# Two attention layers on one core: another order of the running maxima in plain steps, and two loads moved by a step

## The chip, the core and the metric

The kernel runs on one core of a Trainium2 chip. The metric is the device time of one execution, in microseconds (us); a run here means the median over several executions. A core has five engines with queues of their own, which work side by side and wait for one another through semaphores: PE (matmuls; its weight loads are shown as PEld), DVE (reductions and elementwise work), ACT (activation functions), POOL (elementwise work) and SP, which here issues nearly all of the DMAs. [...]

## The reference

Two attention layers, each over 2048 positions with 576 features, 32 heads of 18. Layer A looks at 8 positions behind each query, every second one; layer B is full attention. The outputs stand side by side.

```python
def _A_ref(x, wqkv, wo):
    B, S, D = x.shape
    H = 32; Dh = D // H
    W, dil = 8, 2
    qkv = (lambda x, *d: x.transpose(*d))((x @ wqkv).reshape(B, S, 3, H, Dh), 2, 0, 3, 1, 4)
    q, k, v = qkv[0], qkv[1], qkv[2]
    scale = Dh ** -0.5
...
    idx = pos[:, None] - off[None, :]
...
    logits = jnp.einsum("bhsd,bhswd->bhsw", q, kg) * scale
    logits = jnp.where(mask[None, None, :, :], logits, -1e9)
    attn = _softmax(logits, axis=-1)
    o = jnp.einsum("bhsw,bhswd->bhsd", attn, vg)
    return (lambda x, *d: x.transpose(*d))(o, 0, 2, 1, 3).reshape(B, S, D) @ wo

def _B_ref(x, wqkv, wo):
...
    scores = jnp.einsum("bhqd,bhkd->bhqk", q, k) * scale
    p = _softmax(scores, axis=-1)
    o = jnp.einsum("bhqk,bhkd->bhqd", p, v)
    return (lambda x, *d: x.transpose(*d))(o, 0, 2, 1, 3).reshape(B, S, D) @ wo
...
return jnp.concatenate([a, b], axis=-1)
```

## The kernel before

The first 420 us compute the projections (q, k, v of both layers) and the first 516 of 2048 maximum matmuls. After that the program is a loop of 512 steps, written out by hand. The 32 heads of layer B are taken in 8 groups g of four heads; a group has 4 blocks of 512 queries; a block has 16 steps, one for each 128 keys. Block n = 4 g + b begins at step 16 n. The work of a step:

- **Four scores** (`score`, line 305): for head h of the group a matmul of 56 rows, 128 keys against 512 queries. Head h uses the rows 64 r to 64 r + 55 of the array with r = h mod 2, so that two scores run side by side on the two row groups. Each score writes one of four PSUM banks ("scores"); ACT takes the exponential out of it into a tile `e` (line 309).
- **The weighing** (`weigh`, line 772) of the step before: four matmuls of the values with `e`, in two passes each, which use all rows and sum into the bank `po`. After 16 steps the sums leave through `finish`.
- **Maxima for later blocks.** The softmax needs the largest score of each query before its exponentials, so the same scores are computed ahead of time the other way round (queries on the partitions) and reduced by DVE. A *whole* maximum (`whole`, letters A for row group 0 and B for row group 1) is a matmul of 512 columns (line 175) into one of three PSUM banks ("else") and a reduction by DVE (lines 191 and 193). A *half* maximum (`part` through `first_part`, letters D and E) is done in a pair: D writes 256 columns of row group 0 into a bank, E writes 256 columns of row group 1 into the other half of the same bank, and one reduction (line 205) reads both. E's matmul stands behind a no-operation on PE (line 201) that waits until D's matmul is through.

What a step does in which order is a string: digits are scores, letters the maxima. Where nothing else is due, the step is *plain* and the string is `PLAIN` (line 50). Where local results are multiplied with their output weights (`sums_of_a`, lines 1104 on), there are four whole maxima and another order. PE works its queue in this order; the weighing follows the eight matmuls of the string.

When the last of a block's 64 maximum matmuls has been reduced (at step s), the maxima go on by an agenda of due steps: `least` (DVE, line 214) at s, `turn` (a transpose on DVE, line 222) at s + 1, `halve` (a split in two parts on POOL, line 112) at s + 2, `order` (line 232: two DMAs to DRAM, `dm<-mt`) two steps after that, and `place` (line 238: two DMAs back into the rows of the queries, `qs<-dm`) three steps later, in the last group one step later. The first score of the block needs them. By the order of the agenda, what was planned at the start stands before what is added on the way.

All these DMAs go through SP's queue, which issues them in the order of the program: an issue that waits for its semaphores holds up all behind it.

Layer A runs on POOL, DVE and ACT beside all this, in 8 portions j of 256 positions (`local`). A portion's results are written to DRAM by `put`, read again in halves n by `get` (lines 990 and 992: six DMAs, `at<-dao` and `ahl<-dao`, into tiles that exist once) and multiplied by `sums_of_a` in two later steps from the list `TURNS`. The step of `get` is the later of the step in which the tiles' last use before comes (or the results are in DRAM), `at`, and nine steps before the first use, `one - 9`.

Of the kernel before, what the change touches and what calls it, by code (L numbers as in the profile page):

```python
# [22 lines left out]
NG = H // 4  # L23
# [23 lines left out]

MORE = (439, 441, 451, 467, 475, 477, 484, 486)

PLAIN = "D1A30E2B"  # L50

GAP = 55

# [10 lines left out]
def rows(t, *dims):  # L64

    return bass.AP(tensor=t.tensor, offset=t.offset, ap=[list(d) for d in dims])
# [3 lines left out]
def two_attentions(ctx: ExitStack, tc, xa, wa, woa, xb, wb, wob, out):  # L70
# [19 lines left out]
    def bank(kind=None):  # L90
        r = rings[kind or ring]
        r.append(r.pop(0))
        return p_bank.tile([128, 512], F32, name=f"bank{r[-1]}")
# [17 lines left out]
    def split_on(engine, hi, lo, raw):  # L111
        engine.tensor_copy(hi, raw)  # L112
        engine.tensor_sub(lo, raw, hi)
# [5 lines left out]
    def later(n, f):  # L119
        agenda[step + n].append(f)  # L120
# [37 lines left out]
    def behind_of(later, *before):  # L158

        for b in before:  # L160
            tc.add_manual_dep(later.ins, b.ins.name,
                              mybir.DependencyInfo(mybir.DependencyClass.Sync, mybir.DependencyReason.DATA),
                              reason="in order")

    def block(g, b):

        qs, ks = sets[g % 3]
        mx = maxes.tile([128, 2, 2, 4, 6], F32, name="mx", bufs=3)
        left = 2 * 8 * 6
        rest = [[(k, t, p) for k in range(NB) for t in range(4) for p in range(2)] for _ in range(2)]  # L170

        def take(ps, r, k, t, p, at, n):

            rows_ = slice(64 * r, 64 * r + 54)
            return nc.tensor.matmul(ps, qs[rows_, b, p, 128 * t : 128 * t + 128],  # L175
                                    ks[rows_, p, 512 * k + at : 512 * k + at + n], start=True, stop=True)

        def made(n):
            nonlocal left
            left -= n  # L180
            if left == 0:
                later(int(projecting), least)

        def whole(r):
            k, t, p = rest[r].pop(0)
            ps = bank()
            take(ps, r, k, t, p, 0, 512)

            def reduce():
                if k < 2:  # L190
                    nc.vector.tensor_reduce(mx[:, r, p, t, k : k + 1], ps, axis=AX.X, op=ALU.max)  # L191
                else:
                    nc.vector.tensor_reduce(mx[:, r, p, t, 2 * k - 2 : 2 * k], ps.rearrange("q (h n) -> q h n", h=2),  # L193
                                            axis=AX.X, op=ALU.max)
                made(1 + (k > 1))

            return reduce

        def part(i, k, t, p, r, ps, before=None):
            if before:  # L200
                behind_of(nc.tensor.nop(nofuse=True), before)
            ins = take(ps[:, 256 * r : 256 * r + 256], r, k, t, p, 256 * i, 256)

            def reduce():
                nc.vector.tensor_reduce(mx[:, :, p, t, 2 * k - 2 + i], ps.rearrange("q (h n) -> q h n", h=2),  # L205
                                        axis=AX.X, op=ALU.max)
                made(2)

            return ins, reduce

        def least():
            m = least_rooms[n_least[0] % 2]
            n_least[0] += 1
            nc.vector.tensor_reduce(m[:, :16], mx.rearrange("q r p t k -> q (r p t) k"), axis=AX.X, op=ALU.max,
                                    negate=True)
            later(1, lambda: turn(m))

        def turn(m):

            parts = maxes.tile([128, 2, 32], F32R, name="mt", bufs=2)  # L220
            raw = parts[:, 1].bitcast(F32)
            nc.vector.transpose(raw, m)  # L222
            later(1, lambda: halve(parts, raw))

        def halve(parts, raw):
            split_on(nc.gpsimd, parts[:, 0], parts[:, 1], raw)
            later(2, lambda: order(parts))

        def order(parts):

            for k in range(2):
                load(rows(dm[g, b, k, 0, 0], (32, 4), (128, 32), (1, 32)), parts[:, k].bitcast(F32))
            later(1 if g == NG - 1 else 3, place)

        def place():
            placed.add((g, b))
            for k in range(2):
                load(qs.bitcast(F32)[54 + k : 128 : 64, b].rearrange("r p n -> r (p n)"),
                     dm[g, b, k, :16].rearrange("(r i) n -> r (i n)", r=2))

        return rest, whole, part
# [169 lines left out]
    with (tc.tile_pool(name="x", bufs=1, side="right") as xp,  # L411
# [103 lines left out]
        if True:  # L515
# [34 lines left out]
            for c in range(5):  # L550
                one, other = (load, nc.scalar.dma_start) if c % 2 == 0 else (nc.scalar.dma_start, load)
# [159 lines left out]
            for k in range(2, 14):  # L711
                n = 46 if k == 2 else 36 + 4 * k
# [7 lines left out]
            def leave_a(c, b, n, ps):  # L720
                o = xp.tile([128, 512], F32, name="ohi", bufs=4)
                nc.scalar.activation(o[:n], ps, AF.Copy)  # L722
                load(da[128 * c : 128 * c + n, HALO + 512 * b : HALO + 512 * b + 512], o[:n])


            order = [t for i in (0, 8) for j in range(4) for t in (i + j, i + j + 4)]
# [18 lines left out]
            order = [(c, b) for b0 in range(0, NB, 2) for c in range(2) for b in (b0, b0 + 1)]  # L745
            order += [(c, b) for c in range(2, 14) for b in range(NB)]
            for c, b in order:
                n = min(128, 3 * D - 128 * c)
                work_list.append(((b % 2, ws[c][0], xas[b][0], slice(0, n), every),
                                  lambda ps, n=n: ps[:n], lambda ps, c=c, b=b, n=n: leave_a(c, b, n, ps)))  # L750
# [135 lines left out]
    def local(j):  # L886
# [92 lines left out]
        def put(i):  # L979
            load(rows(dao[j, i, 0, 0], (DH * SUB, 128), (1, DH * SUB)),  # L980
                 ap(st["parts"][i].bitcast(F32), (1, DH * SUB)))

        def get(n):
            st["x"] = []
            st["n"] = n
            last = work.tile([128, 128], F32R, name="ahl", bufs=1)
            for i in range(2):
                t = work.tile([128, 4, 128], F32R, name=f"at{i}", bufs=1)
                for s in range(2):
                    load(t.bitcast(F32)[:, :, SUB * s : SUB * s + SUB],  # L990
                         dao[j, i, 2 * n + s, :512].rearrange("(c p) n -> p c n", p=128))
                load(last.bitcast(F32)[64 * i : 64 * i + 64].rearrange("p (s n) -> p s n", s=2),
                     rows(dao[j, i, 2 * n, 512], (SUB, 64), (D * SUB, 2), (1, SUB)))
                st["x"].append([t[:, c] for c in range(4)])
            st["x"].append(last)

        def finished(h):
            inside.append(lambda: sums_of_a(h))
# [18 lines left out]
        pieces = [(LOWER, lower), (SHARE, share), (UP, upper), (REST, rest), (PUT0, lambda: put(0)), (PUT1, lambda: put(1))]  # L1017
# [12 lines left out]
        start = A_FROM + GAP * j  # L1030
        for n in range(2):
            free, begin = turns[-1] if turns else 0, start + PUT1 + 5
            at = max(free, begin)
            one = next(t for t in TURNS if t >= at + 7)
            two = next(t for t in TURNS if t > one + 1)
            turns.extend((one, two))
            pieces.append((max(at, one - 9) - start, lambda n=n: get(n)))
            for h, t in enumerate((one, two)):
                pieces.append((t - 1 - start, lambda h=h: finished(h)))
                producing.add(t)  # L1040
            pieces.append((two + 5 - start, lambda n=n: load(out[p0 + 128 * n : p0 + 128 * n + 128, :D], ys["a", j, n])))
# [142 lines left out]
    for j in range(NJ):  # L1184
        plan(A_FROM + GAP * j, local(j))
# [40 lines left out]
    while step < ALL:  # L1226
        n, kt = divmod(step, NT)
        g, b = divmod(n, NB)
        many = min(4 if behind() > 0 else 3, total - int(sum(given)))
        if not inside and many in (1, 3):  # L1230
            order = PLAIN if many > 1 else PLAIN.replace("A", "").replace("B", "")
        else:
            places = positions(many)
            order = "".join("%d%s" % (h, "BA"[h % 2] if h in places else "") for h in range(4))
            if inside:
                at = order.index("3" if 3 in places else "2") if step % NT != AT or AT == 0 else FIRST
                order = order[:at] + "+" + order[at:]
# [56 lines left out]
```

## Time and profile before

| what | value |
|---|---|
| median of three runs | 1611.54 us (1610.16 to 1611.78) |
| the profiled execution, its own time | 1610.11 us |
| its span, first to last instruction | 1608.3 us |
| busy share of PE, DVE, ACT, POOL | 99%, 86%, 75%, 60% |
| granted TensorE clock | 0.999 |

The profile comes from one execution. A row of a timeline has the start and the length in us, the engine, the line of the kernel, the operation, the tiles (out<-in), the shapes and how many were merged; in brackets the idle time before it and what ended that. A row of a group has busy time, mean duration and idle time before. Busy times of PE rest on modelled ends of matmuls.

### The profile page before, as it was taken

The page shows a single profiled execution, that of the slowest core. Times are in us where ns is not written, and L with a number is a line of the kernel's source. Part 1 is how long each engine was busy: PE and PEld are TensorE (multiplying, and loading weights), DVE is VectorE, ACT ScalarE, POOL GpSimd, SP SyncE. Part 2 cuts the span into 40 slices and gives each one's busy share as a digit, 9 for nine tenths or more (in the row PEclk, how much of TensorE's full clock was granted, in tenths as well). Part 3 has the DMA queues.
Part 4 walks back from the last instruction along what each step waited for, and adds up shares of the span by engine and source line. Part 5 has one row for each costly group of instructions (what it writes and reads, how often), then busy time and mean ns, then how long its engine had stood idle before and what let it go on. Part 6 is the DMA issues. An engine that isn't in the chain of part 4 may idle for free.

```text
span 1608.3 us, 34964 instructions
## 1 busy us (share of the span) xinstructions
PE 1597.4 (99%) x13360; PEld 956.0 (59%) x13360; DVE 1388.4 (86%) x2350; ACT 1213.3 (75%) x2421; POOL 962.0 (60%) x816
## 2 busy tenths in 40 slices
PE   9999999999999999999999999999999999999998
PEld 7999999999544444444444444444444444444776
DVE  5199999999999999999999999999999999998533
ACT  6323432121699999999999999999999999997454
POOL 2305742210256997985995994995994996930100
PEclk9999999999999999999999999999999999999999
DMA  8937954532322353164136135323523232234211
GB/s 256 232 125 206 258 181 123 143 105 80 61 58 56 72 114 103 38 132 117 46 90 162 43 83 151 80 63 99 134 60 93 58 85 76 80 122 138 84 39 60
DMA packets 190150, 173.13 MB, mean 108 GB/s; under 512 B 123120, under 2 KB 136944, under 8 KB 188256
## 3 DMA queue, kind: packets, MB, share of 16 engines
q1 hardware_dynamic: 185120, 159.36, 35.8%
q0 software_dynamic: 4032, 10.63, 3.2%
q8 instruction: 106, 1.74, 0.5%
q10 hardware_dynamic: 832, 0.92, 0.2%
q14 instruction: 60, 0.49, 0.1%
HBM read 97.47 MB, written 72.95 MB: 106 GB/s over the span
## 4 chain that ended last, share of the span: by engine, by line
PE 98%; DVE 1%; DMA 0%; SPq 0%; ACT 0%; issue 0%; POOL 0%; ACTq 0%; POOLq 0%; DVEq 0%
PE po L772 31%; PE bank L305 19%; PE bank L175 19%; PE bank L394 17%; PE bank L1104 7%; PE bank L331 5%; DVE mx L191 0%; PE bank L546 0%; DMA qs<-dm 0%; DMA out<-y 0%; DVE mx L193 0%; PE bank L1079 0%; ACT vs L612 0%; DVE rec L843 0%; POOL xlo L442 0%
## 5 line engine op out<-in xcount | busy, mean ns | idle before, releaser
L309 ACT ACTIVATE e<-bank 128x512 f32<-128x512 f32 x2048 | 1047.2, 608 | 58.8 <-PE bank L305 51.8
L175 PE MATMUL bank<-ks,qs 54*128 54x512 f32 (+1 forms) x2502 | 784.0, 381 | 1.0 <-DVE mx L191 0.5
L191 DVE TENSOR_REDUCE mx<-bank 128x1 f32<-128x512 f32 x1024 | 682.6, 685 | 87.7 <-PE bank L175 65.1
L175 PEld LDWEIGHTS bank<-ks,qs 54*128 54x128 f32 x2502 | 398.2, 184 | 431.5 <-DVE mx L205 348.2
L305 PE MATMUL bank<-qs,ks 56*128 56x512 f32 x2048 | 574.5, 426 | 3.4 <-DMA qs<-dm 3.4
L772 PE MATMUL po<-e,v 128*19 128x512 f32 x4096 | 538.3, 600 | 0.0
L193 DVE TENSOR_REDUCE mx<-bank 128x2 f32<-128x512 f32 x570 | 373.4, 685 | 32.8 <-PE bank L175 21.5
L305 PEld LDWEIGHTS bank<-qs,ks 56*128 56x128 f32 x2048 | 302.5, 185 | 45.0 <-ACT e L309 34.4
L205 DVE TENSOR_REDUCE mx<-bank 128x2 f32<-128x512 f32 x454 | 309.7, 682 | 0.0
L962 POOL TENSOR_TENSOR pr<-lg,akv 128x1024 f32<-128x1024 f32 x72 | 157.2, 2205 | 0.6
L772 PEld LDWEIGHTS po<-e,v 128*19 128x19 f32 x4096 | 70.6, 97 | 132.2 <-issue 123.6
L722 ACT ACTIVATE ohi<-bank 128x512 f32<-128x512 f32 (+1 forms) x56 | 30.4, 595 | 154.5 <-issue 101.5
L394 PE MATMUL bank<-xhi,ahi 64*128 64x512 f32 (+1 forms) x448 | 120.2, 390 | 0.0
L394 PE MATMUL bank<-xhi,alo 64*128 64x512 f32 (+1 forms) x448 | 114.1, 390 | 0.0
L394 PE MATMUL bank<-xlo,ahi 64*128 64x512 f32 (+1 forms) x448 | 109.3, 391 | 0.1
L914 POOL TENSOR_TENSOR pr<-aq,akv 128x1024 f32<-128x1024 f32 x40 | 87.9, 2204 | 10.7 <-PE bank L175 9.6
L964 POOL TENSOR_TENSOR pr<-pr 128x512 f32<-128x512 f32 x72 | 91.4, 1292 | 0.6
L442 POOL TENSOR_TENSOR alo<-raw,ahi 128x512 fp32r<-128x512 f32 (+1 forms) x14 | 17.6, 1258 | 111.9 <-ACT ahi L441 100.1
L534 POOL TENSOR_TENSOR olo<-olo,ohi 128x512 fp32r<-128x512 f32 x36 | 46.2, 1297 | 61.9 <-ACT ohi L533 57.3
L917 POOL TENSOR_TENSOR pr<-pr,aohi 128x1024 f32<-128x1024 f32 x32 | 76.6, 2393 | 0.6
L917 POOL TENSOR_TENSOR pr<-pr 128x1024 f32<-128x1024 f32 x32 | 76.4, 2388 | 0.0
L112 POOL CAST mt<-mt 128x32 fp32r<-128x32 f32 x32 | 6.8, 213 | 111.1 <-DVE mt L222 111.1
(200 smaller groups left out, 2093.1 us busy)
## 6 DMA issues: line engine op xcount, KB each, us to landing
do<-n SPq DMA_DIRECT2D x28, 512.0 KB
da<-ohi SPq DMA_DIRECT2D x52, 256.0 KB
akv<-da SPq DMA_DIRECT2D x64, 175.5 KB
out<-y SPq DMA_DIRECT2D x32, 288.0 KB
qs<-dqk SPq DMA_DIRECT2D x30, 288.0 KB
ks<-dqk SPq DMA_DIRECT2D x30, 288.0 KB
at<-dao SPq DMA_DIRECT2D x64, 128.0 KB
rec<-drec SPq DMA_DIRECT2D x29, 256.0 KB
```

The lines of the kernel that those rows point to most:

```text
L175: return nc.tensor.matmul(ps, qs[rows_, b, p, 128 * t : 128 * t + 128], ks[rows_, p, 512 * k + at : 512 * k + at + n], start=True, stop=True)
L191: nc.vector.tensor_reduce(mx[:, r, p, t, k : k + 1], ps, axis=AX.X, op=ALU.max)
L193: nc.vector.tensor_reduce(mx[:, r, p, t, 2 * k - 2 : 2 * k], ps.rearrange("q (h n) -> q h n", h=2), axis=AX.X, op=ALU.max)
L205: nc.vector.tensor_reduce(mx[:, :, p, t, 2 * k - 2 + i], ps.rearrange("q (h n) -> q h n", h=2), axis=AX.X, op=ALU.max)
L305: nc.tensor.matmul(ps, ks[at, p, 128 * kt : 128 * kt + 128], qs[at, b, p], start=True, stop=True)
L309: nc.scalar.activation(e, ps, AF.Exp, scale=SCALE)
L394: nc.tensor.matmul(ps, a, b, start=start, stop=stop)
L772: nc.tensor.matmul(po[32 * i : 32 * i + 19], vs[g][:, kt, 19 * i : 19 * i + 19], es[i], start=kt == 0, stop=kt == NT - 1)
L917: nc.gpsimd.tensor_add(st["prs"][0], st["prs"][0], st["prs"][c - 1])
L962: nc.gpsimd.tensor_mul(at, ap(st["lg"], (0, 2), (SUB, W), (1, SUB)), window(st["v"], n))
L964: nc.gpsimd.tensor_add(at[:, :, :4], at[:, :, :4], at[:, :, 4:])
L1104: nc.tensor.matmul(ps, a, b, start=start, stop=stop)
```

## The change

The string of the plain steps puts A first and D third, B sixth and E last; it was D first, A third, E sixth and B last. The scores stay in the order 1, 3, 0, 2. In the last group `order` comes one step after `halve` where it came two steps after. And `get` comes at the earliest one step after `at`.

```diff
-PLAIN = "D1A30E2B"
+PLAIN = "A1D30B2E"
...
         def halve(parts, raw):
             split_on(nc.gpsimd, parts[:, 0], parts[:, 1], raw)
-            later(2, lambda: order(parts))
+            later(1 if g == NG - 1 else 2, lambda: order(parts))
...
             one = next(t for t in TURNS if t >= at + 7)
             two = next(t for t in TURNS if t > one + 1)
             turns.extend((one, two))
-            pieces.append((max(at, one - 9) - start, lambda n=n: get(n)))
+            pieces.append((max(at + 1, one - 9) - start, lambda n=n: get(n)))
```

## The prediction

> **What bounds the kernel now.** I read the page first, then the timeline of PE, weight loads, ACT and DVE over one plain step, then the waits, and last SP's queue around the one long stall.
>
> ```profile
> span 1608.3 us, 34964 instructions
> PE 1597.4 (99%) x13360; PEld 956.0 (59%) x13360; DVE 1388.4 (86%) x2350; ACT 1213.3 (75%) x2421; POOL 962.0 (60%) x816
> PE 98%; DVE 1%; DMA 0%; SPq 0%; ACT 0%; issue 0%; POOL 0%; ACTq 0%; POOLq 0%; DVEq 0%
> ```
>
> PE fills the chain, but ends of matmuls are modelled, so this does not say that PE is never held up. Here is one plain step, PE in the timeline (start, length, line; 54x256 are the halves D and E, L305 the scores, the other L175 rows A and B, L772 the weighing). "Rows 0" and "rows 1" below are the two row groups that r picks.
>
> ```profile
> 702.64 0.38 PE L175 MATMUL bank<-ks,qs 54*128 54x256 f32 x1
> 702.64 0.50 PE L305 MATMUL bank<-qs,ks 56*128 56x512 f32 x1
> 702.86 0.39 PE L175 MATMUL bank<-ks,qs 54*128 54x512 f32 x1
> 702.98 0.40 PE L305 MATMUL bank<-qs,ks 56*128 56x512 f32 x1
> 703.10 0.40 PE L305 MATMUL bank<-qs,ks 56*128 56x512 f32 x1
> 703.22 0.31 PE L175 MATMUL bank<-ks,qs 54*128 54x256 f32 x1
> 703.33 0.42 PE L305 MATMUL bank<-qs,ks 56*128 56x512 f32 x1
> 703.36 0.40 PE L175 MATMUL bank<-ks,qs 54*128 54x512 f32 x1
> 703.69 1.05 PE L772 MATMUL po<-e,v 128*19 128x512 f32 x8
> 704.67 0.38 PE L175 MATMUL bank<-ks,qs 54*128 54x256 f32 x1
> ```
>
> From the first matmul to the weighing is 1.05 us (702.64 to 703.69), from there to the next step 0.98, together 2.03. The mean step agrees: between these two weighings lie 15 steps, 30.53 us, 2.035 each.
>
> ```profile
> 420.48 0.63 PE L772 MATMUL po<-e,v 128*19 128x512 f32 x4
> 451.01 0.63 PE L772 MATMUL po<-e,v 128*19 128x512 f32 x4
> L175 PE MATMUL bank<-ks,qs 54*128 54x256 f32 x908 | 315.7, 348 | 0.1
> ```
>
> 908 halves are 454 plain steps: 10 ns in each is 4.5 us. What sets the 1.05? The weight loads of E, score 2 and B, ACT's exponentials (score 2 of the step before, score 1 and score 2 of this one) and DVE's maxima:
>
> ```profile
> 703.14 0.18 PEld L175 LDWEIGHTS bank<-ks,qs 54*128 54x128 f32 x1
> 703.26 0.18 PEld L305 LDWEIGHTS bank<-qs,ks 56*128 56x128 f32 x1
> 703.26 0.18 PEld L175 LDWEIGHTS bank<-ks,qs 54*128 54x128 f32 x1
> 702.59 0.62 ACT L309 ACTIVATE e<-bank 128x512 f32<-128x512 f32 x1
> 703.17 0.60 ACT L309 ACTIVATE e<-bank 128x512 f32<-128x512 f32 x1
> 704.62 0.62 ACT L309 ACTIVATE e<-bank 128x512 f32<-128x512 f32 x1
> 703.90 0.68 DVE L205 TENSOR_REDUCE mx<-bank 128x2 f32<-128x512 f32 x1
> 704.50 0.68 DVE L191 TENSOR_REDUCE mx<-bank 128x1 f32<-128x512 f32 x1
> ```
>
> Score 2's load starts at 703.26, 0.05 after ACT has left that score's bank (702.59 + 0.62 = 703.21): it waits for the bank. B's load stands behind it in PE's queue, and the weighing follows 0.43 after. So a **loop through ACT** paces plain steps: score 1 ends 0.50 into the step, ACT begins at 0.53 (703.17), reaches score 2 at 1.98, leaves it at 2.60; 0.05 later the next step's score 2 loads; 0.43 and 0.98 after that another step begins. That is 2.60 + 0.05 + 0.43 + 0.98 = 4.06, two steps of 2.03.
>
> **The order in plain steps.** Same eight matmuls, same bytes, row groups still alternating. Before: rows 0 run D, A, 0, 2 and rows 1 run 1, 3, E, B. After: A, D, 0, 2 and 1, 3, B, E. Scores keep their order, so the loop through ACT stays if score 1 ends as before. A step around local results already begins with a score and a whole maximum:
>
> ```profile
> 684.03 0.50 PE L305 MATMUL bank<-qs,ks 56*128 56x512 f32 x1
> 684.03 0.50 PE L175 MATMUL bank<-ks,qs 54*128 54x512 f32 x1
> 684.37 0.40 PE L175 MATMUL bank<-ks,qs 54*128 54x512 f32 x1
> ```
>
> The first pair ends after 0.50, as now; the next starts at 0.34. So the new step is: A and 1 at 0, D and 3 at 0.34, 0 at about 0.46, B at 0.58 (0.24 after 3, the pitch from 702.86 to 703.10), 2 no earlier than 0.69. What is new is the tail. E may start only when D is through (a nop, L201). Today E's load comes 0.12 after D's end (702.64 + 0.38 = 703.02, then 703.14). A half that does not wait for its load takes 0.31, or 0.28 without the rest of its load, as D's 0.38 holds 0.10 of it; D then ends at 0.62 to 0.65 and E loads at 0.74 to 0.77. From B's load to the weighing are 0.43 (703.26 to 703.69); E has half the columns, 0.09 less (0.40 against 0.31) to 0.12 (half the pitch), so 0.31 to 0.34. The weighing starts at 1.05 to 1.11, against 1.05 now; score 2's own branch gives 0.62 + 0.43 = 1.05. I take 1.05, the lower end, since the row of E is held by its load and the pitch is not: 0 to 1 ns a step, +0.5 us over 454. Both ends for the range: a gain is bounded by ACT's loop, in which score 2's load stays; B's load, which drops out, stands less than 0.01 behind it (both at 703.26), shared by two steps 5 ns, -2.3 us; at most 0.06 lost, +27 us. Behind E waits only the weighing, and behind that all of the next step.
>
> DVE: now E's maximum ends at 704.58 and B's at 705.18, 0.11 before B's bank is wanted again (load at 0.62 in the next step, 705.29). After, A is ready 0.11 earlier (0.50 instead of 703.25 - 702.64 = 0.61), so the last maximum, then E's, ends at 705.07, 0.40 into the next step; B takes that bank and must load by 0.47 (0.58 less the 0.11 of a load). Cover 0.07, less the 0.05 of a signal; D takes B's bank, free long before. Cost 0; each 10 ns that it lacks is 4.5 us.
>
> **The maxima of the last group one step earlier.** This touches four blocks. One of them stalls today: the first step of block 30 (step 480). SP's queue, then PE:
>
> ```profile
> 1453.60 1.23 SPq L232 DMA_DIRECT2D dm<-mt  x2
> 1463.79 0.93 SPq L990 DMA_DIRECT2D at<-dao  x2
> ...
> 1467.98 1.06 SPq L238 DMA_DIRECT2D qs<-dm  x2
> 1468.25 1.05 PE L772 MATMUL po<-e,v 128*19 128x512 f32 x8
> 1472.98 0.47 PE L305 MATMUL bank<-qs,ks 56*128 56x512 f32 x1 [3.36 <-DMA qs<-dm]
> 1479.56 1.05 PE L772 MATMUL po<-e,v 128*19 128x512 f32 x8
> ```
>
> The maxima leave at 1453.60, but their way back (L238) stands behind the fetch of local results (L990), which waits until PE has read the tile's former contents: nine microseconds with nothing issued. PE then waits 3.36 us, and the matmuls behind it are late as well. The three steps from 1468.25 to 1479.56 take 11.31; the same three at the start of block 1 take 6.53:
>
> ```profile
> 448.98 0.63 PE L772 MATMUL po<-e,v 128*19 128x512 f32 x4
> 455.51 1.05 PE L772 MATMUL po<-e,v 128*19 128x512 f32 x8
> ```
>
> By the code, block 30 is complete at step 472, its maxima are stored (order) at 476 and loaded (place) at 477, in the same step as the fetch get(7, 1) and listed behind it. After, order is at 475 and place at 476 (a step earlier still, since counting the pieces in the new order completes the block at 471), and the fetch at 478. So L238 passes L990. What it waits for then is the way to DRAM, which took 2.3 us for block 29 (first two rows); the third is the landing of the stalled load, from the chain of waits:
>
> ```profile
> 1413.89 1.28 SPq L232 DMA_DIRECT2D dm<-mt  x2
> ...
> 1416.22 1.12 SPq L238 DMA_DIRECT2D qs<-dm  x2
> 1468.56 4.28 DMA qs<-dm
> ```
>
> Issued by 1457, landed 4.3 us later, by 1462, wanted at 1469: the stall goes whole, **-4.8 us** (11.31 - 6.53). Bounds: nothing if it stays behind, -4.8 if all goes. What SP carries past is two stores and two loads; the six fetches behind them start at 1463.79 either way, since PE's reading releases them; their first use is at step 484. The other three blocks' loads are not waited for today: 0.
>
> **The fetch a step later.** Of 16 fetches five move: those at steps 105, 215, 368, 467 and 477. Their results are wanted 6 steps or more after the new place, 12 us, against 8.5 for the six issues and a landing (1463.79 to 1467.98 is 4.2; a landing 4.3, if it takes as long as the stalled one): 0. If that cover were gone, one step's 2 us each.
>
> **Sum.** +0.5 - 4.8 + 0 + 0 = -4.3 us. The profiled execution took 1610.11 (span 1608.3), so 1605.8 for such a one; the median 1611.54 lies 1.43 higher, so **1607.2** for the median.
>
> **Rivals.** (1) Slower: the **tail through the nop decides**. From the point where E's load to the weighing ends later than score 2's branch (1.05), each further ns costs 0.45 us; over 10 ns it eats the 4.8. With 25 ns, the middle of 0 to 0.06 taken low, 11.4 - 4.8 = +6.6: 1618. For it: E's load, held by the nop, would be the last thing before the weighing; against: the estimate meets 1.05 at its lower end. (2) **No net change**: some 10 ns a step (nop, or DVE's 0.02 of cover) against the 4.8, or SP's load still late: 1611.5. (3) **Faster by more**: if the loop through ACT did not bind, the tail would be shorter by B's delay behind score 2, 0.03 (703.33 to 703.36), 454 x 0.03 = 13.6: 1593. Against it: the 0.05 between ACT's end and the load.
>
> (4) Weights loaded only beside other rows: if E's load had to wait for B on the same rows, it would start at 0.58 + 0.24 = 0.82, the weighing at 1.13 to 1.16, at least +0.08 a step, 36 us: 1643. Against it: E's load at 703.14 starts while score 3 on the same rows runs (702.98 to 703.38). [...]
>
> **How the numbers follow.** The forecast 0.60, rival 1 0.17, rival 2 0.13, rival 3 0.07, rival 4 0.03. About 0.2% (3.2 us) is what a measurement of this kernel tells from no change. Faster than 1608.3: 0.55 of the forecast and rival 3, 0.62; within: the rest of the forecast and rival 2, 0.18; slower: rivals 1 and 4, 0.20. Range 1603 to 1615: the forecast with its bounds, rival 2 and the lower half of rival 1, which leaves out about 0.19. The forecast's own range is 1604 to 1610.
>
> **What would show it.** The chain has no qs<-dm piece near 1468, and L238 stands before L990 there. Plain steps stay at 2.035, score 2's load 0.05 behind ACT. It is wrong if the distance from first matmul to weighing leaves 1.05, with E's load as the last before it at over 0.75, or if the maxima on DVE hold B's load.

## The result, and the profile after

The changed kernel takes 1608.91 us (median of 20 runs) against 1611.45 us for the kernel before (20 runs): a ratio of 0.9987 (95% interval 0.998 to 0.9994), 2.5 us less. The profiled execution took 1608.64 us. Forecast were 1607.2 us, 4.3 less. The head of its page:

```profile
span 1606.9 us, 34967 instructions
PE 1598.9 (100%) x13360; PEld 987.9 (61%) x13360; DVE 1390.0 (87%) x2350; ACT 1216.0 (76%) x2421; POOL 961.4 (60%) x816
PE 98%; DVE 1%; DMA 0%; ACT 0%; issue 0%; POOL 0%; ACTq 0%; POOLq 0%; DVEq 0%
```

The engines' shares say nothing new. Two places do. The first is SP's queue ahead of step 480, from the timeline of SP, and then PE's weighings of steps 479 and 482, from the timeline of PE:

```profile
1455.65 1.96 SPq L232 DMA_DIRECT2D dm<-mt  x2
1463.60 1.14 SPq L238 DMA_DIRECT2D qs<-dm  x2
...
1467.34 0.92 SPq L990 DMA_DIRECT2D at<-dao  x2
1471.81 1.05 PE L772 MATMUL po<-e,v 128*19 128x512 f32 x8
...
1478.36 0.63 PE L772 MATMUL po<-e,v 128*19 128x512 f32 x4
```

L238, the way back of the maxima, now stands ahead of L990, the fetch of local results. The three steps take 6.55 us instead of 11.31: the stall is gone, and 4.8 us with it. The maxima's way to DRAM was slower than forecast: L238 waited for it, as the waits of SP between 1450 and 1475 us say (the columns are total, times, longest).

```profile
SPq L238 <- DMA dm<-mt: 5.9, 1, 5.9
```

It waited 5.9 us, and the whole way took 8.0 (1455.65 to 1463.60) where block 29 took 2.3. The loads are issued at 1463.60 and not by 1457; the step that needs them begins at 1472.80. If they land 4.3 us later, as the prediction took, they are there some 5 us early instead of 7, so this costs nothing here.

The second place is the plain step. From the timelines of PE, the weight loads, ACT and DVE, one step of the changed kernel (A, score 1; then scores 3 and 0 in one row, B, score 2, E):

```profile
668.70 0.49 PE L175 MATMUL bank<-ks,qs 54*128 54x512 f32 x1
668.70 0.49 PE L305 MATMUL bank<-qs,ks 56*128 56x512 f32 x1
669.04 0.51 PE L305 MATMUL bank<-qs,ks 56*128 56x512 f32 x2
669.27 0.40 PE L175 MATMUL bank<-ks,qs 54*128 54x512 f32 x1
669.38 0.46 PE L305 MATMUL bank<-qs,ks 56*128 56x512 f32 x1
669.51 0.30 PE L175 MATMUL bank<-ks,qs 54*128 54x256 f32 x1
669.78 0.63 PE L772 MATMUL po<-e,v 128*19 128x512 f32 x4
669.14 0.18 PEld L175 LDWEIGHTS bank<-ks,qs 54*128 54x128 f32 x1
669.35 0.18 PEld L305 LDWEIGHTS bank<-qs,ks 56*128 56x128 f32 x1
669.43 0.18 PEld L175 LDWEIGHTS bank<-ks,qs 54*128 54x128 f32 x1
668.68 0.62 ACT L309 ACTIVATE e<-bank 128x512 f32<-128x512 f32 x1
669.26 0.60 ACT L309 ACTIVATE e<-bank 128x512 f32<-128x512 f32 x1
668.40 0.68 DVE L205 TENSOR_REDUCE mx<-bank 128x2 f32<-128x512 f32 x1
669.23 0.69 DVE L191 TENSOR_REDUCE mx<-bank 128x1 f32<-128x512 f32 x1
```

Score 2's weights load at 669.35, 0.05 after ACT has left their bank (668.68 + 0.62 = 669.30): ACT's loop still sets the pace. E's load comes 0.08 later, at 0.73 into the step, and is not what the weighing waits for: 669.43 and the 0.31 of the prediction make 669.74, and the weighing starts at 669.78, 0.43 after score 2's load. (In about a third of the plain steps the weighing does stand 0.31 behind E's load; it then comes at about 1.05 into the step, as before.)

But A and score 1 both end at 668.70 + 0.49 = 669.19. DVE takes A's bank at 669.23, 0.04 later; ACT takes score 1's at 669.26, **0.07 later**. In the step of before it was 0.03 (703.14 to 703.17): score 1 stood second there too, but D beside it had ended 0.12 earlier (703.02). The ends of matmuls are modelled, so the rows alone cannot say whether score 1 ended later or was reported later. The trace also records when PE's semaphore goes up, which the views do not print: here at 669.207 and at 669.241, and ACT starts 0.023 after the second. In all 502 pairs of a maximum and a score in this trace that start and end together, the two signals stand 0.034 or 0.035 apart. These 0.03 us lie in the loop of two steps, so 15 ns in each. The mean says 12: between these two weighings lie 15 steps in 30.71 us, 2.047 each, where it was 2.035.

```profile
420.47 0.63 PE L772 MATMUL po<-e,v 128*19 128x512 f32 x4
...
451.18 0.62 PE L772 MATMUL po<-e,v 128*19 128x512 f32 x4
```

### The profile page after: what moved, and what is told of

It is laid out like the page before. It is cut to its first block, busy times and chain, and to the rows that moved or that the text cites. A ratio compares the mean times of both kernels' runs of the same rounds, so it can differ in the third digit from the quotient of the medians.

```text
span 1606.9 us, 34967 instructions
## 1 busy us (share of the span) xinstructions
PE 1598.9 (100%) x13360; PEld 987.9 (61%) x13360; DVE 1390.0 (87%) x2350; ACT 1216.0 (76%) x2421; POOL 961.4 (60%) x816
## 4 chain that ended last, share of the span: by engine, by line
PE 98%; DVE 1%; DMA 0%; ACT 0%; issue 0%; POOL 0%; ACTq 0%; POOLq 0%; DVEq 0%
PE po L772 32%; PE bank L175 25%; PE bank L394 15%; PE bank L305 14%; PE bank L1104 7%; PE bank L331 5%; DVE mx L191 0%; DMA first<-xb 0%; DMA out<-y 0%; PE bank L1079 0%; ACT vs L612 0%; DVE rec L843 0%; POOL xlo L442 0%; DVE mx L193 0%; DVE wlo L442 0%
## 5 line engine op out<-in xcount | busy, mean ns | idle before, releaser
L191 DVE TENSOR_REDUCE mx<-bank 128x1 f32<-128x512 f32 x1024 | 655.7, 684 | 83.5 <-PE bank L175 39.3
L175 PEld LDWEIGHTS bank<-ks,qs 54*128 54x128 f32 x2502 | 423.0, 184 | 399.7 <-DVE mx L191 275.3
L305 PE MATMUL bank<-qs,ks 56*128 56x512 f32 x2048 | 580.6, 429 | 0.0
L193 DVE TENSOR_REDUCE mx<-bank 128x2 f32<-128x512 f32 x570 | 363.9, 685 | 33.4 <-PE bank L305 12.9
L305 PEld LDWEIGHTS bank<-qs,ks 56*128 56x128 f32 x2048 | 329.9, 184 | 71.9 <-ACT e L309 35.2
L205 DVE TENSOR_REDUCE mx<-bank 128x2 f32<-128x512 f32 x454 | 309.6, 682 | 0.0
L394 PE MATMUL bank<-xhi,ahi 64*128 64x512 f32 (+1 forms) x448 | 114.4, 390 | 0.0
L394 PE MATMUL bank<-xhi,alo 64*128 64x512 f32 (+1 forms) x448 | 108.6, 390 | 0.0
L394 PE MATMUL bank<-xlo,ahi 64*128 64x512 f32 (+1 forms) x448 | 103.5, 391 | 0.1
```

The costliest lines, as they stand in the source:

```text
L305: nc.tensor.matmul(ps, ks[at, p, 128 * kt : 128 * kt + 128], qs[at, b, p], start=True, stop=True)
L394: nc.tensor.matmul(ps, a, b, start=start, stop=stop)
```

## The experiments

The theory after these two readings: the loads moved in SP's queue bring some 5 us, and the string of the plain steps gives a part of it back, since the matmul that stands second of a pair that ends together told its reader 0.034 us later here (**theory 1**, signals). The rivals: the string is neutral and the stall was worth less (theory 2); DVE holds the bank that B wants (theory 3); the nop in front of E sets the tail (theory 4). All runs are compared with the kernel before on the same chip, 1611.32 us (e1, e2, e3, e5) and 1611.29 us (e4, e6, e7). The changed kernel was not run again beside them; where a run is compared with its 1608.91, the kernel before, 1611.45 us beside it, is what links the two.

**e1_sp_only**: the edits to the loads, with the string of before.

```diff
-PLAIN = "A1D30B2E"
+PLAIN = "D1A30E2B"
```

(This and the diffs for e3, e6 and e7 are against the changed kernel.)

> The string of before, with the store of the maxima (order) a step earlier in the last group and the fetch a step later. Theory 1 (signals): the stall at step 480 goes, -4.8 us, and plain steps stay at 2.035 us; score 1's exponential starts 0.037 us after its matmul: about 1606.7, 2.3 us less than the changed kernel. Theory 2 (the two loads are worth only what the changed kernel shows, and the string is neutral): about 1609, as the changed kernel.

Measured: 1605.62 us, ratio 0.9965 (0.9953 to 0.9978). The loads alone bring 5.7 us; the changed kernel is 3.3 us slower than this. The new string costs time; theory 2 falls.

**e2_plain_only**: the string alone, against the kernel before.

```diff
-PLAIN = "D1A30E2B"
+PLAIN = "A1D30B2E"
```

> The new string alone; order and the fetch as before. Block 30 completes a step earlier by the new string, so its load (place) is due at step 476, ahead of the fetch at 477. Theory 1: the stall goes without the other two edits, and plain steps take about 2.048 us: 1609, as the changed kernel. Theory 2 (the stall goes only by the edits to the loads; the string is neutral): 1611.5, as before. If the string costs 5 us and the stall stays: 1616.

Measured: 1609.55 us, ratio 0.999 (0.9981 to 0.9999), as the changed kernel within the intervals. The stall is gone here too:

```profile
1456.09 2.82 SPq L232 DMA_DIRECT2D dm<-mt  x2
1464.56 1.14 SPq L238 DMA_DIRECT2D qs<-dm  x2
1467.67 0.92 SPq L990 DMA_DIRECT2D at<-dao  x2
```

That is SP's timeline of this kernel: L238 ahead of L990 with neither edit to the loads, because the new string completes block 30 a step earlier: its `least` (L214) starts behind the 471st weighing, and behind the 472nd in the kernel before. With it, the two other edits have nothing left to remove.

**e3_score_first**: score 1 ahead of A.

```diff
-PLAIN = "A1D30B2E"
+PLAIN = "1AD30B2E"
```

> The changed kernel with score 1 ahead of A in the string (1AD30B2E), all else equal. Theory 1: the pair still ends together, but score 1 signals first; ACT starts 0.037 us after its matmul instead of 0.068, A's maximum starts 0.03 later, which nothing waits for; plain steps 2.034 us instead of 2.048: about 1604, 5 us less than the changed kernel. Theory 3 (DVE holds B's bank: B's weight load waits for E's maximum and that lengthens the step): A's maximum is later, so the step is as long or longer: 1609 or more. Theory 4 (the nop in front of E sets the tail): unchanged, 1609.

Measured: 1604.65 us, ratio 0.9959 (0.9946 to 0.9971), 4.3 us less than the changed kernel. From the timelines of PE, ACT and DVE of this kernel, the pair and its readers, and again two weighings 15 steps apart:

```profile
443.77 0.50 PE L305 MATMUL bank<-qs,ks 56*128 56x512 f32 x1
443.77 0.49 PE L175 MATMUL bank<-ks,qs 54*128 54x512 f32 x1
444.30 0.60 ACT L309 ACTIVATE e<-bank 128x512 f32<-128x512 f32 x1
444.34 0.69 DVE L191 TENSOR_REDUCE mx<-bank 128x1 f32<-128x512 f32 x1
420.41 1.05 PE L772 MATMUL po<-e,v 128*19 128x512 f32 x8
...
450.92 0.63 PE L772 MATMUL po<-e,v 128*19 128x512 f32 x4
```

Now ACT starts 0.03 after its matmul (443.77 + 0.50 = 444.27) and DVE 0.08 after its own (444.26): the two have changed places. PE's semaphore goes up at 444.278 and 444.313, and ACT starts 0.023 after the first. The step is 30.51 / 15 = 2.034 us. E is still last and A's maximum is later, so neither the nop nor DVE made the changed kernel slow; theories 3 and 4 do not explain it, theory 1 does.

**e5_order_only**: the maxima stored a step earlier in the last group, against the kernel before.

```diff
-            later(2, lambda: order(parts))
+            later(1 if g == NG - 1 else 2, lambda: order(parts))
```

> The kernel of before with order a step earlier in the last group alone; the string and the fetch as before. The load of block 30's maxima is due at step 476, ahead of the fetch at 477. If the place in SP's queue is all that counts: the stall goes whole, about 1606.7. If the fetch a step later is needed as well: 1611.5.

Measured: 1606.41 us, ratio 0.9969 (0.9957 to 0.9981). Alone it removes the stall.

**e4_fetch_only**: the fetch a step later, against the kernel before.

```diff
-            pieces.append((max(at, one - 9) - start, lambda n=n: get(n)))
+            pieces.append((max(at + 1, one - 9) - start, lambda n=n: get(n)))
```

> The kernel of before with the fetch a step later alone; the string and order as before. The fetch comes at step 478, behind the load of block 30's maxima at 477. If the place in SP's queue is all that counts: the stall goes whole, 1606.5, as with order alone. If the load has to be earlier: the stall stays in part, 1608 to 1611.5.

Measured: 1605.35 us, ratio 0.9965 (0.9951 to 0.9979): so does this one alone. SP's timeline:

```profile
1453.71 1.23 SPq L232 DMA_DIRECT2D dm<-mt  x2
...
1460.49 1.10 SPq L238 DMA_DIRECT2D qs<-dm  x2
1463.92 0.92 SPq L990 DMA_DIRECT2D at<-dao  x2
```

The fetch loses nothing: it starts when PE has read the tile, at 1463.92 here and at 1463.79 before.

**e6_half_late**: score 1 first as in e3, and D in sixth place, so that the nop in front of E waits longer.

```diff
-PLAIN = "A1D30B2E"
+PLAIN = "1A30BD2E"
```

> The kernel with score 1 first, with D moved to sixth place (1A30BD2E); the same work. Tests the tail through the nop: D then starts at about 0.58 and ends at 0.85, E's weights load 0.12 later at 0.97, and the weighing starts 0.31 after that at 1.28 instead of 1.05: 0.23 us in each of some 430 plain steps, about 1700. If the nop's wait is not what holds E (its weights go in early, or the weighing does not wait for E): 1605 to 1610.

Measured: 1766.78 us, ratio 1.0966 (1.0951 to 1.0981), more than expected. PE and its weight loads (the step begins at 737.34; the second row holds B and D):

```profile
737.34 0.50 PE L305 MATMUL bank<-qs,ks 56*128 56x512 f32 x1
737.90 0.40 PE L175 MATMUL bank<-ks,qs 54*128 54x512 f32 x2
738.45 0.18 PEld L175 LDWEIGHTS bank<-ks,qs 54*128 54x128 f32 x1 [0.36 <-issue]
738.76 1.05 PE L772 MATMUL po<-e,v 128*19 128x512 f32 x8
```

The last part is as expected: from E's load to the weighing 0.31. The load itself comes at 1.11 into the step, not at 0.97. It follows B's end (737.90 + 0.40 = 738.30) by 0.15, and D, the shorter one, started together with B but stands behind it. So the wait for D was over only after B's end: D's signal came behind B's (PE's semaphore goes up at 738.314 and at 738.348). These 0.14 us in 454 steps are 64 us, nearly all that the expectation of 1700 lacked. The tail through the nop was a real cost here with D in sixth place; in the changed kernel, where D stands third, it stays within the 1.05.

**e7_half_second**: score 1 first, D second and A third, E last.

```diff
-PLAIN = "A1D30B2E"
+PLAIN = "1DA30B2E"
```

> The kernel with score 1 first, with D second and A third (1DA30B2E): score 1 ends beside a half and signals alone, E stays last. Theory 1 alone (score 1's signal and ACT's loop): 1605, as with 1AD30B2E. With DVE's loop as well: A's maximum is ready 0.11 later, E's, the last, ends 0.51 into the next step instead of 0.40, and B's weights wait for its bank; the loop B's load to weighing 0.55, on to the next step 0.98, A's maximum at 0.65, two more and 0.68 to its end closes at 2.065 us a step, 0.03 more: about 1617.

Measured: 1613.95 us, ratio 1.0019 (1.0011 to 1.0028), 9.3 us more than with A second. DVE's maximum of E, B's weight load in the next step, and that step's weighing:

```profile
700.80 0.68 DVE L205 TENSOR_REDUCE mx<-bank 128x2 f32<-128x512 f32 x1
701.54 0.18 PEld L175 LDWEIGHTS bank<-ks,qs 54*128 54x128 f32 x1
702.08 0.62 PE L772 MATMUL po<-e,v 128*19 128x512 f32 x4
```

B's weights load 0.06 after DVE has left the bank (701.48), and the weighing follows 0.54 later, as the loop through DVE asks. Half of the plain steps of this trace take 2.067 us or more, against 2.065 expected. In the changed kernel B's load stands 0.06 behind DVE as well (668.40 + 0.68 = 669.08, load at 669.14), but the weighing comes 0.64 after it, behind score 2: the loop through DVE had some 0.1 us to spare there. The median is less than the 1617 expected; the profiled execution was one of 1616.24. That steps which are long for another reason do not pay again would explain a smaller total, but was not tried.

## Why the prediction was right, and what was mis-sized

- **The stall (-4.8 us)**: right in place, cause and size. The three steps fell from 11.31 to 6.55 us, and the two edits together brought 5.7, each alone 4.9 and 5.9. The medians give up to 1 us more than the rows; this was not resolved. That either edit, or the string alone, is enough the prediction half said: it counted the completion of block 30 a step earlier, but booked the gain to the loads.
- **The way to DRAM ("issued by 1457, landed by 1462")**: wrong by 6.6 us, without consequence. At block 29, the last of eight loads of 252 KB in the same queue had been issued 11 us before the maxima left; here the last of eight such loads was issued 3 us before. That these made it slow was not tried.
- **The fetch a step later (0)**: right.
- **The new string (+0.5 us)**: the term that was mis-sized. It measured 3.3 us (1608.91 against 1605.62), or 3.9 on the chip of e1 and e2 (1609.55 against 1605.62, neither with the stall). The step that failed reads "Scores keep their order, so the loop through ACT stays if score 1 ends as before", with "The first pair ends after 0.50, as now". Score 1 does end as before, but ACT hears of it 0.03 later, since A ends with it and stands ahead of it. The loop that the prediction had added up to 4.06 us is then 4.09, 2.045 a step where 2.047 was measured. That would be about 5 us over 454 steps; the mean of all plain steps in the traces rises by 9 ns (2.055 in e1, 2.064 in the changed kernel), 4 us, so not every plain step pays the whole.
- **The nop's tail and DVE's cover (0)**: right. E's load came at 0.73 (forecast 0.74 to 0.77), and 0.31 behind it is the 1.05 that was forecast. E's maximum ended 0.38 into the next step (forecast 0.40), so B's matmul starts at 0.57 (forecast 0.58); but B's load stands 0.05 to 0.06 behind DVE in 85% of the plain steps, where it did so in 3% before. It loads at 0.44 and must by 0.47, so the cover is as thin as forecast. e6 and e7 show what each costs when its cover is gone.
- **The rivals**: the "no net change" rival had the right shape, a string that costs some 10 ns a step against the 4.8, but named the nop or DVE for it. The slower tail, the missing loop and the weights that load only beside other rows did not come about; against the last, E's load at 669.43 starts while B runs on the same rows (669.27 to 669.67).
- **The total**: -4.3 was forecast and -2.5 measured. The string cost 3 us more than its term and the stall brought about 1 us more, so the two misses offset in part, and the range was wide enough for the rest: that is luck and not the mechanism. The result, 1608.91, lies in the band that the prediction gave 0.18, not below 1608.3, where it had put 0.62. Of its signs, L238 ahead of L990, the chain without a qs<-dm piece near 1468 and score 2's load 0.05 behind ACT came; plain steps did not stay at 2.035, and the distance to the weighing left 1.05 (1.08 in the step shown), with E's load at 0.73 and score 2's branch deciding.

In the trace of the changed kernel PE's semaphore goes up for A and score 1, which end together, one after the other, 34 ns apart (669.207 and 669.241). Here the place in the pair decided which reader paid them.

## What to carry to other kernels

When matmuls on two row groups end together, as A and score 1 did here with 0.034 us between their signals, put first the one whose reader lies on the loop that sets the pace: swapping two letters was worth 4.3 us here, with the same work. Before costing a new order, add up the loop through the engines, signals included, and ask of each signal what ends at the same moment. And where a stall stands in a DMA queue that is worked in the order of the program, as SP's here (L990 waited 9.2 us for PE, with L238 behind it), look for the transfer in front that waits for something else: passing it once was enough here (4.9 and 5.9 us for either edit alone, 5.7 for both), and the second edit that did the same added nothing.

## What the hardware showed beyond that

In the changed kernel, of two matmuls that ended together the second in the queue reported 0.034 or 0.035 us after the first. In e6 the wait for D ended only when B, ahead of it, had ended: with D beside and behind B, E's load came 0.15 us after B's end (738.30, load at 738.45), where in the kernel before it came 0.12 after D's end (703.02, load at 703.14), with D ending alone. And a small transfer's way to DRAM took 2.3 us at block 29 in the kernel before and 8.0 at block 30 in the changed one (1455.65 to 1463.60).

The fastest version run is the changed kernel with score 1 ahead of A, 1604.65 us. Against the string of before with the same loads, 1605.62, it gains 1.0 us, of which the step explains some 0.5 (2.034 against 2.035, 454 steps), and no more than the intervals can tell. In this version the weighing stands 0.31 behind E's load in 82% of the plain steps, at 1.05: the tail through the nop is now level with the loop through ACT.
